# Loading q in one transfer with 32 token groups outermost, in a fused retention and token-mixing kernel

## The chip, the cores and the metric

The kernel runs on one core of one Trainium2 chip. The metric is the device time of one execution in microseconds (us), as the median of several runs. A separate execution was taken by the hardware profiler; its rows are used to see where the time goes.

## What is computed

Inputs are q, k and v, each of shape 4 x 8 x 768 x 64 (batch, heads, tokens, head width) in 32-bit floats, and three weights. All of q, k and v are 6.29 MB each.

```python
# retention: one decaying 64x64 state per batch and head
for t in range(S):
    state = gamma[h] * state + outer(k[:, :, t], v[:, :, t])
    y[:, :, t] = q[:, :, t] @ state / sqrt(D)
x = y.transpose(0, 2, 1, 3).reshape(B, S, H * D)      # 4 x 768 x 512
# token mixing: the weights over tokens come from x itself
W_tok = (x @ w_q) @ (x @ w_k).T / sqrt(d_hyper)        # per batch, no softmax
out = relu(W_tok @ x) @ w_out                          # 4 x 768 x 512
```

Because there is no softmax, the kernel forms `z = (x @ w_k).T @ x` per batch and multiplies `x @ w_q` with it.

## The kernel before

The work is cut into 12 pairs. A pair is 256 tokens of one batch, two chunks (c = 0, 1) of 128 tokens, and three pairs make a batch. For each pair the steps are: loads of k, v and q; casts to bf16 (`ck`, `cv` with the decay multiplied in, `cq`); transposes of k and q on TensorE into PSUM (`trk`, `trq`) and their evictions (`ek`, `eq`); scores k times q (`sc`), evicted with a causal mask (`eat`); the product with v (`ia`); the product of q with the carried state (`in`, `ic`); the state update (`st`, `es`); the eviction of y with its decay (`ex`); the transpose of x (`xt`, `exT`); the products with w_q and w_k (`wqk`, evicted by `ew`); z (`zm`, `ez`); the mix (`mx`, relu in `r`); the output projection (`pj`, evicted by `eo`); and the store.

Two lists written out by hand set the order. `ORDER` lists every step with its engine (A is ScalarE, V is VectorE, P is GpSimd) and its PSUM bank, and each engine runs its own steps strictly in that order. `LOADS` lists the transfers in the order in which SyncE issues them, all but the first half of k of pair 0: first the loads of all pairs, then all stores. A staging pool has 16 buffers of 512 KB; the load that reuses a buffer waits until the tensor before it is cast. The q of a pair is the 2nd, 5th, 6th, ... entry, and the last loads are `k11 q11 v10 v11`.

A q load (line 151) is two transfers, one for the even and one for the odd heads. In each, the four heads of that parity are outermost, then 32 groups of 8 neighbouring tokens, then 8 x 64 floats, which are 2 KB in a row in DRAM. So partition 32 w + g holds head pair w and token group g. The k and v loads (lines 159 and 167) have 128 token groups or tokens outermost, with rows of 512 bytes (types 1 and 2) or 256 bytes (type n, the last three pairs). After `trq`, eight transposes of 128 x 128, the columns of the transposed q come in the order (w, c, j, group), with j the token within its group, so that each head pair's 128 tokens of a chunk lie in a row for the score matmuls. Tokens are then handled in the order (j, group) in all later steps, and a store (line 823) writes 128 rows of 2 KB per chunk with the 8 values of j outermost, one transfer for each chunk.

The transposed q has two uses on TensorE: as the moving operand of the scores (lines 496 and 514), and as the stationary operand, loaded as weights, of the products with the state (lines 554, 580 and 599).

Of the kernel before, what the change touches and what calls it, by code (L numbers as in the profile page):

```python
# [10 lines left out]
BF16 = mybir.dt.bfloat16  # L11
# [56 lines left out]
def kernel(  # L68
# [13 lines left out]
    nc = tc.nc  # L82
# [3 lines left out]
    DH = moe_w_q.shape[1]  # L86
    C = 128
# [4 lines left out]
    HP = H // 2  # L92
    J = 8
    QG = C // J

    wk_scale = (1.0 / math.sqrt(D)) ** 3 / math.sqrt(DH)
# [3 lines left out]
    def pool(name, bufs, **kw):  # L100
        return ctx.enter_context(tc.tile_pool(name=name, bufs=bufs, **kw))
# [7 lines left out]
    kq_pool = pool("kq", KQS)  # L109
# [9 lines left out]
    def bank32(b, n=1):  # L119
        return banks[:, b : b + n, :].rearrange("p n f -> p (n f)")  # L120

    def bank16(b):
        return banks[:, b, :].bitcast(BF16)

    pairs = [dict() for _ in range(NG)]
# [4 lines left out]
    ENGINES = {"A": nc.scalar, "V": nc.vector, "P": nc.gpsimd}  # L130

    def copy(e, out, in_):
        if e == "A":
            return nc.scalar.copy(out=out, in_=in_)  # L134
        return ENGINES[e].tensor_copy(out=out, in_=in_)  # L135

    def rows(i):
        return slice(i * 64, i * 64 + 64)

    def halves(half):  # L140
        return slice(0, HP) if half is None else slice(half * HP // 2, (half + 1) * HP // 2)

    def load(name, p, half=None, eng=None):
        src = {"k": k, "q": q, "v": v}[name]
        b, cp = divmod(p, NP)
        st = pairs[p]
        t0 = cp * 2 * C
        if name == "q":
            st["q_st"] = stage_pool.tile([128, 2, J, D], FP32, name="q_st", tag="st")
            for x in range(2):  # L150
                nc.sync.dma_start(  # L151
                    out=st["q_st"][:, x].rearrange("p j d -> p (j d)"),
                    in_=src[b, x::2, t0 : t0 + 2 * C, :].rearrange("w (g j) d -> w g (j d)", j=J),
                )
            return
        if TYPES[p] == "n":
            st[name + "_st"] = stage_pool.tile([128, 2, HP, 2, D], FP32, name=name + "_st", tag="st")
            for c in range(2):
                (eng or nc.sync).dma_start(  # L159
                    out=st[name + "_st"][:, c].rearrange("t hp x d -> t (hp x) d"),  # L160
                    in_=src[b, :, t0 + c * C : t0 + (c + 1) * C, :].rearrange("h t d -> t h d"),
                )
            return
        if name + "_st" not in st:
            st[name + "_st"] = stage_pool.tile([128, HP, 2, 2, D], FP32, name=name + "_st", tag="st")
        hs = halves(half)
        (eng or nc.sync).dma_start(
            out=st[name + "_st"][:, hs].rearrange("g hp x j d -> g (hp x) (j d)"),
            in_=src[b, 2 * hs.start : 2 * hs.stop, t0 : t0 + 2 * C, :].rearrange(
                "h (g j) d -> g h (j d)", j=2  # L170
            ),
        )

    wstages = {}
# [18 lines left out]
    def load_token(token):  # L193
        if token[0] in "wo":
            load_weights(token)
        else:
            load(token[0], int(token[1:]))

    load("k", 0, 0, nc.scalar)
    load("k", 0, 1, nc.sync)  # L200

    queue = list(LOADS)
# [19 lines left out]
    def release(token, n):  # L222
        parts[token] = parts.get(token, 0) + 1
        if parts[token] == n:
            cast.add(token)
            more_loads()
# [14 lines left out]
        out=pt[:, 1:2], in0=pt[:, 0:1], scalar1=4, scalar2=None, op0=ALU.arith_shift_right  # L241
    )
    nc.vector.tensor_scalar(
        out=pt[:, 2:3], in0=pt[:, 0:1], scalar1=15, scalar2=3,
# [19 lines left out]
    for x in range(2):  # L264
# [11 lines left out]
        out=ty.rearrange("p n x c h -> p (n x c h)"),  # L276
        in0=ty.rearrange("p n x c h -> p (n x c h)"),
# [7 lines left out]
    if "2" in TYPES:  # L285
        fy2 = const_pool.tile([128, NP, 2, HP, 2], FP32, name="fy2")
        for cp in range(NP):
            nc.vector.tensor_copy(
                out=fy2[:, cp], in_=fy[:, cp].rearrange("p x c hp -> p c hp x")
            )  # L290

    if "n" in TYPES:
# [10 lines left out]
            out=tn.rearrange("p n c h -> p (n c) h"),  # L303
            in0=tn.rearrange("p n c h -> p (n c) h"),
# [32 lines left out]
    wqk_sb = const_pool.tile([128, NDM, 3 * DH], BF16, name="wqk_w")  # L337
    wout_sb = const_pool.tile([128, NDM, DM], BF16, name="wout_sb")

    def W(e):  # L340
        copy(
            e,
            wqk_sb[:, :, 0 : 2 * DH].rearrange("p a (r h) -> p a r h", r=2),
            wstages["w"][:, 0][:, :, None, :].to_broadcast([128, NDM, 2, DH]),
        )
        wk_stage = wstages["w"][:, 1]
        if e == "A":
            nc.scalar.mul(out=wqk_sb[:, :, 2 * DH :], in_=wk_stage, mul=float(wk_scale))
        else:
            ENGINES[e].tensor_scalar_mul(  # L350
                out=wqk_sb[:, :, 2 * DH :], in0=wk_stage, scalar1=float(wk_scale)
            )
        release("w", 1)

    def WO(e, b, i):
# [114 lines left out]

    def trq(e, b, p):
        st = pairs[p]
        ps = bank16(b).rearrange("p (n j g) -> p n j g", j=J, g=QG)
        for j in range(J):
            nc.tensor.transpose(  # L475
                ps[:, :, j], st["qs"][:, j].rearrange("p x d -> p (x d)"), identity
            )
        st["qT_ps"] = bank16(b)

    def eq(e, b, p):  # L480
        st = pairs[p]
        st["qT"] = kq_pool.tile([128, HP, 2, J, QG], BF16, name="qT")
        copy(e, st["qT"].rearrange("p w c j g -> p (w c j g)"), st["qT_ps"])

    def qT(p, x, hp, c):
        return pairs[p]["qT"][rows(x), hp, c].rearrange("p j g -> p (j g)")

    def sc1(e, b, p, half):
        st = pairs[p]
# [223 lines left out]

    def wqk(e, b, p):
        st = pairs[p]
        wk_ps = bank32(b)[:, 0:128].rearrange("p (c n) -> p c n", c=2)
        wq_ps = bank32(b)[:, 128:384]
        for c in range(2):
            for a in range(NDM):
                nc.tensor.matmul(  # L720
                    out=wk_ps[:, c, :],
                    lhsT=st["xT"][:, a, c, :],
                    rhs=wqk_sb[:, a, 2 * DH :],
                    start=(c == 0 and a == 0),
                    stop=(a == NDM - 1),
                    skip_group_check=True,
                )
        for a in range(NDM):
            nc.tensor.matmul(  # L729
                out=wq_ps,  # L730
                lhsT=wqk_sb[:, a, 0 : 2 * DH],
                rhs=st["xT"][:, a].rearrange("p c t -> p (c t)"),
                start=False,
                stop=(a == NDM - 1),
                skip_group_check=True,
            )
        st["wqk_ps"] = bank32(b)[:, 0:384]

    def ew(e, b, p):
        st = pairs[p]  # L740
        w = moe_pool.tile([128, 384], BF16, name="wqk_n")
        copy(e, w, st["wqk_ps"])
        st["wk"] = w[:, 0:128].rearrange("p (c n) -> p c n", c=2)
        st["wqT"] = w[:, 128:384]

# [69 lines left out]
    def stored(name):  # L815
        p, _, c = name.partition("/")
        p, cs = int(p), [int(c)] if c else [0, 1]
        if not all((p, i) in evicted for i in cs):
            return False
        b, cp = divmod(p, NP)  # L820
        for i in cs:
            t0 = cp * 2 * C + i * C
            nc.sync.dma_start(
                out=out[b, t0 : t0 + C, :].rearrange("(g j) m -> j g m", j=J),
                in_=pairs[p]["o"][:, i],
            )
        return True

    steps2 = dict(
        ck=ck2, cv=cv2, cq=cq, trk=trk, ek=ek, trq=trq, eq=eq, sc=sc2, eat=eat, st=state2, es=es, ia=ia2,  # L830
        **{"in": inter2}, ic=cross2, ex=ex2, xt=xt, exT=exT, wqk=wqk, ew=ew, zm=zm, ez=ez, mx=mx, r=r, pj=pj, eo=eo,
        WO=WO,
    )
# [5 lines left out]
    for token in ORDER:  # L839
        token, _, b = token.partition("@")  # L840
        token, _, e = token.partition(":")
        name, *args = token.split(".")
        args = [int(i) for i in args]
        if name == "fence":
            fence(e, int(b))
        elif name == "fill":
            fill(args[0], int(b))
        elif name == "W":
            W(e)
        elif name == "mask":  # L850
            masks("12n"[args[0]])
        else:
            steps = steps1 if name in ("ez", "WO") else kinds[TYPES[args[0]]]
            steps[name](e, int(b) if b else None, *args)
# [30 lines left out]
```

## Time and profile before

| | |
|---|---|
| median of 3 runs | 152.17 us (152.16 to 152.41) |
| the profiled execution's own time | 153.09 us |
| its span, first to last instruction | 151.4 us |
| TensorE (PE) busy | 97.2 us |
| VectorE (DVE) busy | 75.1 us |
| ScalarE (ACT) busy | 64.1 us |
| GpSimd (POOL) busy | 63.2 us |
| mean granted TensorE clock | 0.80 of full speed |

No engine is busy for two thirds of the span. The granted clock is a share of 2.4 GHz, and a stretch has either 0.5 (1.2 GHz) or 1.0, so means lie between. In the rows, "idle before" is an engine's idle time just ahead of an instruction, with what ended it. The DMA share is the mean busy share of the core's 16 DMA engines, so 0.25 can be four engines at full work, and it can read slightly above 1 in a short window.

### The profile page before, as it was taken

How to read it: one execution, taken by the hardware profiler on the slowest of the kernel's cores; microseconds unless marked ns; L12 is line 12 of the kernel's file. 1: busy time of each engine (PE TensorE's matmuls, PEld its weight loads, DVE VectorE, ACT ScalarE, POOL GpSimd, SP SyncE). 2: the span in 40 equal slices, each digit the busy share in tenths (PEclk: the TensorE clock that was granted, in tenths of full speed). 3: DMA queues.
4: the chain of work that ended last, by engine and by line, in shares of the span. 5: the costliest groups of instructions: out<-in, count | busy, mean ns of one | idle time of the engine just before them, and what ended most of it. 6: DMA issues, size and time to landing. Idle time of an engine off the chain costs nothing. (4 is left out here: it accounts for less than half of the span.)

```text
span 151.4 us, 3451 instructions
## 1 busy us (share of the span) xinstructions
PE 97.2 (64%) x1429; PEld 70.4 (47%) x1439; DVE 75.1 (50%) x107; ACT 64.1 (42%) x101; POOL 63.2 (42%) x87
## 2 busy tenths in 40 slices
PE   6704714582693990899719943994466999999200
PEld 2204613572672880677516632663355777644000
DVE  4008423454764291459629980577050896666000
ACT  4306321614762651358227771471250775534300
POOL 7605970092842941971939425970509400000000
PEclk9965555567558599569999999699786999999975
DMA  3766266466766696562635475955448555555551
GB/s 103 206 187 191 109 187 197 129 224 166 205 197 181 210 296 180 171 191 102 191 115 183 138 209 140 254 147 140 125 145 185 177 194 197 201 199 204 205 204 74
DMA packets 39263, 26.69 MB, mean 176 GB/s; under 512 B 14160, under 2 KB 32592, under 8 KB 39248
## 3 DMA queue, kind: packets, MB, share of 16 engines
q1 hardware_dynamic: 38720, 26.22, 57.3%
q10 hardware_dynamic: 528, 0.26, 0.6%
q8 instruction: 11, 0.18, 0.5%
q14 instruction: 4, 0.03, 0.1%
HBM read 20.19 MB, written 6.29 MB: 175 GB/s over the span
## 5 line engine op out<-in xcount | busy, mean ns | idle before, releaser
L414 POOL TENSOR_TENSOR vs<-v_st,fv 64x512 bf16<-64x512 f32 x24 | 26.6, 1107 | 16.5 <-DMA v_st<-in_v_dram 15.2
L475 PE MATMUL banks<-identity,qs 128*128 128x128 bf16 x96 | 10.1, 269 | 32.4 <-POOL qs L135 17.1
L796 PE MATMUL banks<-wout_sb,relu 128*128 128x512 bf16 x86 | 23.1, 391 | 1.1 <-issue 0.8
L475 PEld LDWEIGHTS <-qs 128*128 128x128 bf16 x96 | 7.7, 122 | 34.7 <-POOL qs L135 18.3
L528 DVE TENSOR_TENSOR at_sb<-banks,cmask 128x1024 bf16<-128x1024 f32 x18 | 21.5, 1217 | 2.5 <-PE banks L496 1.3
L135 POOL CAST qs<-q_st 128x1024 bf16<-128x1024 f32 (+1 forms) x8 | 7.0, 877 | 32.9 <-DMA q_st<-in_q_dram 28.8
L692 DVE TENSOR_TENSOR x_nat<-banks,fy 128x1024 bf16<-128x1024 f32 x10 | 12.2, 1221 | 9.7 <-PE banks L648 9.6
L134 ACT CAST qs<-q_st 128x512 bf16<-128x512 f32 x7 | 4.3, 619 | 29.4 <-DMA q_st<-in_q_dram 29.4
L134 ACT COPY o_st<-banks 128x512 f32<-128x512 f32 x19 | 11.1, 586 | 11.5 <-PE banks L796 11.4
L135 POOL CAST ks<-k_st 64x512 bf16<-64x512 f32 (+1 forms) x21 | 13.4, 643 | 4.3 <-DMA k_st<-in_k_dram 3.7
L451 PE MATMUL banks<-identity,ks 128*128 128x128 bf16 x96 | 11.1, 280 | 6.1 <-POOL ks L135 4.7
L796 PEld LDWEIGHTS <-relu 128*128 128x128 bf16 x96 | 8.6, 101 | 8.9 <-issue 1.4
L451 PEld LDWEIGHTS <-ks 128*128 128x128 bf16 x96 | 8.6, 128 | 8.0 <-POOL ks L135 5.2
L789 ACT ACTIVATE relu<-banks 128x1024 bf16<-128x1024 f32 x9 | 9.2, 1027 | 7.1 <-PE banks L774 7.1
L135 DVE CAST qs<-q_st 128x512 bf16<-128x512 f32 x4 | 1.7, 427 | 18.9 <-DMA q_st<-in_q_dram 18.9
L134 ACT CAST ks<-k_st 64x512 bf16<-64x512 f32 (+2 forms) x12 | 7.8, 652 | 6.5 <-POOL ks L135 5.0
L134 ACT COPY kT<-banks 128x1024 bf16<-128x1024 bf16 x8 | 8.1, 1012 | 5.1 <-PE banks L451 5.1
L134 ACT COPY qT<-banks 128x1024 bf16<-128x1024 bf16 x7 | 7.1, 1011 | 5.9 <-PE banks L475 5.6
L648 PE MATMUL banks<-vs,at_sb 128*128 128x64 bf16 x160 | 9.1, 213 | 0.0
L496 PE MATMUL banks<-qT,kT 64*128 64x128 bf16 x160 | 8.5, 248 | 0.8 <-DVE qT L135 0.8
L704 PE MATMUL banks<-identity,x_nat 128*128 128x128 bf16 x96 | 8.9, 247 | 0.0
L729 PE MATMUL banks<-xT,wqk_w 128*128 128x256 bf16 x48 | 8.3, 302 | 0.0
(80 smaller groups left out, 164.2 us busy)
## 6 DMA issues: line engine op xcount, KB each, us to landing
q_st<-in_q_dram SPq DMA_DIRECT2D x24, 256.0 KB
out_dram<-o_st SPq DMA_DIRECT2D x24, 256.0 KB
v_st<-in_v_dram SPq DMA_DIRECT2D x9, 512.0 KB
k_st<-in_k_dram SPq DMA_DIRECT2D x8, 512.0 KB
k_st<-in_k_dram SPq DMA_DIRECT2D x7, 256.0 KB
v_st<-in_v_dram SPq DMA_DIRECT2D x6, 256.0 KB
o_st<-in_moe_w_out_dram SPq DMA_DIRECT2D x2, 512.0 KB
k_st<-in_k_dram ACTq DMA_DIRECT2D x1, 256.0 KB
```

What stands on the lines that cost most here:

```text
L134: return nc.scalar.copy(out=out, in_=in_)
L135: return ENGINES[e].tensor_copy(out=out, in_=in_)
L414: ENGINES[e].tensor_tensor(out=st["vs"][rows(j), c].rearrange("p hp x d -> p (hp x) d"), in0=st["v_st"][rows(c), :, :, j].rearrange("p hp ...
L451: nc.tensor.transpose(ps[:, hp, i], src.rearrange("p x d -> p (x d)"), identity)
L475: nc.tensor.transpose(ps[:, :, j], st["qs"][:, j].rearrange("p x d -> p (x d)"), identity)
L496: nc.tensor.matmul(out=ps[:, x, hi, c, :], lhsT=st["kT"][rows(x), hp, c, :], rhs=qT(p, x, hp, c), start=(hi == 0 and c == 0), stop=(hi == ...
L528: ENGINES[e].tensor_tensor(out=st["at", half].rearrange("p x hi i t -> p (x hi i t)").rearrange("p (m n) -> p m n", n=n), in0=st["at_ps", ...
L648: nc.tensor.matmul(out=y[:, x, c, hp, :], lhsT=st["at", half][:, x, hi, c, :], rhs=st["vs"][:, c, hp, x, :], start=first(p, x), stop=False ...
L692: nc.vector.tensor_tensor(out=st["x"].rearrange("p c hp x d -> p x (c hp) d"), in0=st["y_ps"].rearrange("p x c hp d -> p x (c hp) d"), in1 ...
L704: nc.tensor.transpose(ps[:, a, c], st["x"][:, c, a].rearrange("p x d -> p (x d)"), identity)
L789: nc.scalar.activation(out=dst, in_=st["mx_ps"], func=ACT.Relu)
L796: nc.tensor.matmul(out=bank32(b), lhsT=st["relu"][:, a, c, :], rhs=wout_sb[:, a, :], start=(a == 0), stop=(a == NDM - 1),)
```

## The change

The two q transfers become one, with the 32 token groups outermost and the eight heads behind them. Partition 4 g + w then holds token group g and head pair w. The transposed q comes out in the order (c, j, group, w): the four head pairs are interleaved, and the columns of one head pair stand four bf16 elements (8 bytes) apart. The evictions in `eq` stay contiguous copies, while the score matmuls and the state products read the transposed q with that step.

The eviction `ew` writes the tokens back into natural order, reading PSUM with a step of 16 floats. For wk this goes with a reordering of the columns of w_k in `W` and an output of eight-float pieces in `wqk`. The stores then write tokens in natural order: 128 tokens outermost, and both chunks in one transfer for pairs 0 to 8, where 24 store transfers become 15.

```diff
--- before.py
+++ after.py
@@ -147,11 +147,10 @@
         t0 = cp * 2 * C
         if name == "q":
             st["q_st"] = stage_pool.tile([128, 2, J, D], FP32, name="q_st", tag="st")
-            for x in range(2):
-                nc.sync.dma_start(
-                    out=st["q_st"][:, x].rearrange("p j d -> p (j d)"),
-                    in_=src[b, x::2, t0 : t0 + 2 * C, :].rearrange("w (g j) d -> w g (j d)", j=J),
-                )
+            nc.sync.dma_start(
+                out=st["q_st"].rearrange("p x j d -> p x (j d)"),
+                in_=src[b, :, t0 : t0 + 2 * C, :].rearrange("h (g j) d -> g h (j d)", j=J),
+            )
             return
         if TYPES[p] == "n":
             st[name + "_st"] = stage_pool.tile([128, 2, HP, 2, D], FP32, name=name + "_st", tag="st")
@@ -343,13 +342,12 @@
             wqk_sb[:, :, 0 : 2 * DH].rearrange("p a (r h) -> p a r h", r=2),
             wstages["w"][:, 0][:, :, None, :].to_broadcast([128, NDM, 2, DH]),
         )
-        wk_stage = wstages["w"][:, 1]
+        wk_stage = wstages["w"][:, 1].rearrange("p a (h1 h0) -> p a h0 h1", h0=J)
+        wk_sb = wqk_sb[:, :, 2 * DH :].rearrange("p a (h0 h1) -> p a h0 h1", h0=J)
         if e == "A":
-            nc.scalar.mul(out=wqk_sb[:, :, 2 * DH :], in_=wk_stage, mul=float(wk_scale))
+            nc.scalar.mul(out=wk_sb, in_=wk_stage, mul=float(wk_scale))
         else:
-            ENGINES[e].tensor_scalar_mul(
-                out=wqk_sb[:, :, 2 * DH :], in0=wk_stage, scalar1=float(wk_scale)
-            )
+            ENGINES[e].tensor_scalar_mul(out=wk_sb, in0=wk_stage, scalar1=float(wk_scale))
         release("w", 1)
 
     def WO(e, b, i):
@@ -470,7 +468,7 @@
 
     def trq(e, b, p):
         st = pairs[p]
-        ps = bank16(b).rearrange("p (n j g) -> p n j g", j=J, g=QG)
+        ps = bank16(b).rearrange("p (c j n) -> p c j n", c=2, j=J)
         for j in range(J):
             nc.tensor.transpose(
                 ps[:, :, j], st["qs"][:, j].rearrange("p x d -> p (x d)"), identity
@@ -479,11 +477,11 @@
 
     def eq(e, b, p):
         st = pairs[p]
-        st["qT"] = kq_pool.tile([128, HP, 2, J, QG], BF16, name="qT")
-        copy(e, st["qT"].rearrange("p w c j g -> p (w c j g)"), st["qT_ps"])
+        st["qT"] = kq_pool.tile([128, 2, J * QG, HP], BF16, name="qT")
+        copy(e, st["qT"].rearrange("p c t w -> p (c t w)"), st["qT_ps"])
 
     def qT(p, x, hp, c):
-        return pairs[p]["qT"][rows(x), hp, c].rearrange("p j g -> p (j g)")
+        return pairs[p]["qT"][rows(x), c, :, hp]
 
     def sc1(e, b, p, half):
         st = pairs[p]
@@ -713,7 +711,7 @@
 
     def wqk(e, b, p):
         st = pairs[p]
-        wk_ps = bank32(b)[:, 0:128].rearrange("p (c n) -> p c n", c=2)
+        wk_ps = bank32(b)[:, 0:128].rearrange("p (h0 c h1) -> p c h0 h1", h0=J, c=2)
         wq_ps = bank32(b)[:, 128:384]
         for c in range(2):
             for a in range(NDM):
@@ -739,7 +737,11 @@
     def ew(e, b, p):
         st = pairs[p]
         w = moe_pool.tile([128, 384], BF16, name="wqk_n")
-        copy(e, w, st["wqk_ps"])
+        copy(
+            e,
+            w.rearrange("p (i g j) -> p i g j", i=3, j=J),
+            st["wqk_ps"].rearrange("p (i j g) -> p i g j", i=3, j=J),
+        )
         st["wk"] = w[:, 0:128].rearrange("p (c n) -> p c n", c=2)
         st["wqT"] = w[:, 128:384]
 
@@ -818,11 +820,13 @@
         if not all((p, i) in evicted for i in cs):
             return False
         b, cp = divmod(p, NP)
-        for i in cs:
-            t0 = cp * 2 * C + i * C
+        if c:
+            t0 = (2 * cp + cs[0]) * C
+            nc.sync.dma_start(out=out[b, t0 : t0 + C, :], in_=pairs[p]["o"][:, cs[0]])
+        else:
             nc.sync.dma_start(
-                out=out[b, t0 : t0 + C, :].rearrange("(g j) m -> j g m", j=J),
-                in_=pairs[p]["o"][:, i],
+                out=out[b, cp * 2 * C : (cp + 1) * 2 * C, :].rearrange("(c t) m -> t c m", c=2),
+                in_=pairs[p]["o"],
             )
         return True
```

## Rows read from the trace of the kernel before

**Rows 1.** The page: busy time of each engine, and TensorE's clock in 40 slices.

```profile
PE 97.2 (64%) x1429; PEld 70.4 (47%) x1439; DVE 75.1 (50%) x107; ACT 64.1 (42%) x101; POOL 63.2 (42%) x87
...
PEclk9965555567558599569999999699786999999975
```

**Rows 2.** The chain that ended last: start us, us, what.

```profile
105.84 7.84 DMA q_st<-in_q_dram
...
113.83 1.05 POOL qs L135
...
140.87 0.59 ACT o_st L134
```

**Rows 3.** Waits: engine, line, releaser; us in total, times, longest.

```profile
PE banks L475 <- POOL qs L135: 17.1, 5, 4.4
...
PE banks L475 <- ACT qs L134: 9.0, 2, 5.7
...
PE banks L475 <- DVE qs L135: 6.3, 2, 3.3
...
PE banks L451 <- POOL ks L135: 4.7, 2, 4.0
```

**Rows 4.** The q staging tile: idle time of casting engines, and what ended it.

```profile
  DMA q_st<-in_q_dram: 77.2, 17
```

**Rows 5.** Windows of 1 to 1.4 us: busy, clock, DMA share, GB/s.

```profile
53.00:54.00 1.00, 1.00 (x21) 0.95 (x20) 1.00 (x2) 0.00 (x0) 0.94 (x2) 0.91 1.05 332
91.00:92.00 1.00, 0.00 (x0) 0.00 (x0) 0.00 (x0) 0.00 (x0) 0.00 (x0) 1.00 0.27 90
93.00:94.00 1.00, 0.57 (x9) 0.56 (x10) 0.00 (x0) 0.00 (x0) 0.67 (x2) 1.00 1.03 236
146.00:147.00 1.00, 0.00 (x0) 0.00 (x0) 0.00 (x0) 0.00 (x0) 0.00 (x0) 0.50 0.52 203
150.00:151.40 1.40, 0.00 (x0) 0.00 (x0) 0.00 (x0) 0.00 (x0) 0.00 (x0) 0.50 0.00 0
```

**Rows 6.** SyncE's queue late on: start us, us, line, transfer, count.

```profile
102.52 3.85 SPq L151 DMA_DIRECT2D q_st<-in_q_dram  x2
106.47 7.97 SPq L159 DMA_DIRECT2D v_st<-in_v_dram  x4
```

**Rows 7.** Windows by stage; columns PE, PEld, DVE, ACT, POOL, clock, share, GB/s.

```profile
6.70:11.60 4.90, 0.00 (x0) 0.00 (x0) 0.00 (x0) 0.00 (x0) 0.02 (x1) 0.71 0.64 173
11.60:113.80 102.20, 66.31 (x1082) 51.97 (x1088) 56.41 (x63) 46.67 (x71) 52.68 (x59) 0.76 0.61 175
80.00:90.00 10.00, 8.75 (x165) 6.01 (x164) 9.46 (x10) 8.30 (x15) 5.64 (x6) 1.00 0.52 164
113.80:141.46 27.66, 25.45 (x332) 16.55 (x336) 16.90 (x18) 14.25 (x24) 5.09 (x5) 0.94 0.57 195
141.46:151.40 9.94, 0.00 (x0) 0.00 (x0) 0.00 (x0) 0.00 (x0) 0.00 (x0) 0.70 0.40 154
```

**Rows 8.** ScalarE's timeline at the start: k's first load and its cast.

```profile
0.79 0.48 ACTq L167 DMA_DIRECT2D k_st<-in_k_dram  x1
...
5.06 1.24 ACT L134 CAST ks<-k_st 64x512 bf16<-64x512 f32 x2 [1.23 <-DMA k_st<-in_k_dram]
```

**Rows 9.** Groups by form: busy us, mean ns of one, idle before.

```profile
L451 PE MATMUL banks<-identity,ks 128*128 128x128 bf16 x96 | 11.1, 280 | 6.1 <-POOL ks L135 4.7 <-ACT qT L134 1.1 <-ACT ks L134 0.4
...
L475 PE MATMUL banks<-identity,qs 128*128 128x128 bf16 x96 | 10.1, 269 | 32.4 <-POOL qs L135 17.1 <-ACT qs L134 9.0 <-DVE qs L135 6.3
...
L496 PE MATMUL banks<-qT,kT 64*128 64x128 bf16 x160 | 8.5, 248 | 0.8 <-DVE qT L135 0.8
...
L720 PE MATMUL banks<-wqk_w,xT 128*128 128x64 bf16 x96 | 5.6, 208 | 0.0
...
L134 ACT CAST wqk_n<-banks 128x384 bf16<-128x384 f32 x11 | 5.1, 481 | 3.5 <-PE banks L729 3.3
...
L554 PEld LDWEIGHTS <-qT 64*128 64x128 bf16 x128 | 3.7, 109 | 0.7 <-issue 0.2
...
L514 PE MATMUL banks<-qT,kT 64*64 64x128 bf16 x64 | 1.8, 266 | 0.1
```

## The prediction

> **What bounds the kernel now.** I read the page first. PE, the busiest engine, works 97.2 us of a span of 151.4, and its clock falls to half in many slices [rows 1], so something starves all engines at once. The chain of waits names it: the last q lands at 113.7, is cast at 113.83, and from there the work runs without a hole to the last eviction, which ends at 140.87 + 0.59 = 141.46 [rows 2]. The waits say how often this happens. PE stands still ahead of the q transposes nine times, for 17.1 + 9.0 + 6.3 = 32.4 us, and its largest other stall is 4.0 us for a k cast on POOL (`ck.10`), which is queued behind the cast of q [rows 3]. The casting engines waited 17 times for q's data, 77.2 us in all [rows 4].
>
> Why q is late is seen in short windows [rows 5]. At 53 to 54 us all 16 DMA engines are busy and move 332 GB/s. At 91 to 92 every compute engine waits for a q, the DMA share is 0.27 and 90 GB/s flow: four engines. At 146 to 147 only stores are left, with a share of 0.52 and 203 GB/s: eight engines, 25 GB/s each. The count follows the outermost dimension of the access pattern: the four heads of one parity in a q load, the eight j in a store, 128 in the k and v loads. The sum by engine agrees. All of q's 6.29 MB passes through four engines, 1.57 MB each; the stores add 6.29/8 = 0.79 and the rest 13.9/16 = 0.87. That makes 3.23 MB on each of these four, 127 us at 25.4 GB/s, which fills most of the span, while an engine outside the first eight carries 0.87 MB. SyncE's queue is backed up behind them: two q issues take 3.85 us, four v issues 7.97 [rows 6], so k and v come late as well.
>
> **The change, part by part.** *The q load.* With 32 groups outermost on one side and 128 partitions on the other, I expect 16 engines, as 4, 8 and 128 gave 4, 8 and 16. No row shows a load with 32, so four engines stays a rival. With q and the stores spread, each engine carries 26.5/16 = 1.66 MB. One issue in place of two also removes 12 instructions from SyncE's queue; I count nothing for that, since its time is waiting for room.
>
> Three gains follow. First, the start. From 6.7 to 11.6 us no compute engine works [rows 7], waiting for q0. The first k, 0.52 MB in two halves, is issued at 0.79 and cast at 5.06 [rows 8]. A q of 0.52 MB behind it needs 1.6 us at 332 GB/s or 2.2 at 236, the slowest rate of a window with all engines busy [rows 5], so 6.7 to 7.3. I take 7.0, a gain of 4.6.
>
> Second, the stretch from q0's cast to q11's, 102.2 us [rows 7]. If data is there in time, PE loses its stalls for q: 32.4 less the first of 5.7, which is in the gain above, is 26.7, and the 4.0 for `ck.10` makes 30.7. It leaves 71.5 us. In it PE would be busy 66.3, most of it priced at a clock of 0.76, DVE 56.4, POOL 52.7 and ACT 46.7 [rows 7]. So DVE works 79% of the time. What is late next is DVE (score masks, evictions of y) and PE's waits for it. The best that rows allow is DVE's densest stretch, 9.46 of 10 us: 56.4/0.946 = 59.6, which is 11.9 less. I keep 71.5: it takes away only PE's stalls for q, and gains from a warmer PE are set against waits that now come to light.
>
> Are the loads then in time? Up to q11 the loads are 20.2 - 1.05 = 19.1 MB (v10 and v11 follow). Behind k0, at 332 GB/s they end 56 us after 5.06, at 61; at 236 GB/s 79 us after, at 84. The forecast wants q11 at 7.0 + 71.5 = 78.5, so they fit at any rate above 253 GB/s. The low end is a rival below.
>
> Third, the tail. From the last eviction at 141.46 to the end pass 9.94 us [rows 7], because stores still queue on eight engines. With loads done by 80 and 16 engines, the 6.29 MB of stores need 16 us at twice 203 GB/s, during the 27.7 us that PE works after q11's cast, which I leave as they are. The last store of 256 KB then goes alone. Its price is that of the first loads, 5.06 - 0.79 = 4.3, and the 1.4 us at the end in which nothing moves [rows 5]: 5.7, a gain of 4.2.
>
> *The interleaved q.* Where `qT` is the moving operand there are 224 score matmuls, busy 8.5 + 1.8 = 10.3 us. Where it is loaded as weights, 128 loads take 3.7, so all 176 take 5.1 [rows 9]. No row shows PE reading with a step. Below nothing is excluded, since the columns are as many; above I set a doubling, fully exposed: 15.4 us. I take nothing, being nearest to the same instructions as they stand, and keep 15.4 for the range. The Trainium skill's page "SBUF — State Buffer", section "Door 1: The DMA port swizzle", says that SBUF has 16-byte lines and that two hits on a line suffice for full bandwidth. A step of 8 bytes gives just two, so by it the price is nothing; no run here shows it yet.
>
> *PSUM writes in pieces.* `trq` now writes runs of 64 bf16 in place of 16, and the 96 matmuls of `wqk` for wk write runs of eight floats. The row for pieces exists: `trq` in runs of 32 bytes takes 269 ns against 280 for `trk`, which writes whole rows [rows 9]. So I price it at nothing. The Trainium skill speaks against this part: the page "PSUM — Partial Sum Buffer", section "Specifications (TRN2)", says that any non-contiguous access slows matmuls significantly. The two rows do not bear that out for runs of 32 bytes; doubling the 5.6 us of line 720 by it would add 5.6 and give 118.3.
>
> *`ew` and `W`.* Twelve evictions of 481 ns now read with a step. Doubled, they add 5.8 us, nearly all to ACT, which works 64.1 us [rows 1, 9] of some 112; nothing of it is on the path as long as ACT has that slack. `W`'s product runs once on POOL, ahead of work that waits for loads: nothing.
>
> **The sum.** 151.4 - 4.6 - 30.7 - 4.2 = 111.9 us of span. The profiled execution took 153.09, 1.69 more than its span, and the median of the runs is 0.92 below that, so I add 0.77: 112.7.
>
> **The rivals.**
> - *The loads stay the bound.* If the mix of 256- and 512-byte rows holds the 16 engines at 236 GB/s throughout, q11 lands at 84 in place of 78.5, and the end comes 5.3 us later: 118. For it speaks that the 12.6 MB of k and v come in such rows; against it that windows with all engines busy also show 332.
> - *The step costs PE twice.* 112.7 + 15.4 = 128. Against it: PE has 5 us free in the stretch, and some would be hidden.
> - *Slower.* The step costs so much that PE becomes the bound by itself. The gain to be eaten is 152.2 - 112.7 = 39.5 us over 400 instructions, 99 ns each; a score matmul now has 46 ns of busy time and a load 29. At four times the price they add 30.9 + 15.3 = 46.2, and the time is 159. Nothing in the trace speaks for it, and nothing excludes it.
> - *The load stays on four engines.* Then only the tail gains its 4.2 us: 148. Against it: the counts of 4, 8 and 16.
>
> **How the numbers follow.** The forecast's case, with DVE and PE the next bound and 101 to 118 as its own range (from 112.7 - 11.9), gets 0.70. The loads at their low rate get 0.12, the doubled step 0.10, four engines 0.04, slower 0.04. The predicted time is 112.7. The range reaches from 101 to 128, which takes in the second and third; past it lie the last two and some of the first. All cases but the last are faster: 0.95. A change within 0.2%, about what these runs can tell from none, gets 0.01, and slower 0.04.
>
> **What the profile afterwards would show.** Right: no window with a share near 0.27 while all engines wait; DMA at 250 GB/s or more until the loads end at 60 to 85 us; PE's idle time ahead of line 475 below 10 us; under 6.5 us after the last eviction; lines 496 and 554 at their old durations per clock; `trq` no dearer. Wrong would be: q windows still at a quarter of the engines; line 496 or 554 at twice its time; or new waits of PE for DVE or POOL that eat the 30.7 us, the likeliest way to miss within the range's upper half.

## The result, and the profile after

The median falls from 152.29 us (4 runs, 152.16 to 153.25) to 103.27 (4 runs, 101.66 to 105.57), a ratio of 0.670 with a 95% interval of 0.663 to 0.678. All ratios here are of the fast runs alone, without those over 1.5% above the fastest of the same kernel, so that they differ a little from the quotient of the medians (0.678). The profiled execution took 102.75 us with a span of 101.0. The forecast was 112.7 with a range of 101 to 128: the direction and the range hold, with the measured time near the range's lower end, and the gain is 49.0 us where 39.6 were forecast.

The page of the changed kernel answers to [rows 1]: busy time of each engine, TensorE's clock and the DMA share in 40 slices, the chain that ended last by engine, and, from its last part, the q loads and the stores of one chunk (count, size, median us from issue to landing).

```profile
PE 90.5 (90%) x1439; PEld 64.5 (64%) x1439; DVE 75.4 (75%) x107; ACT 63.7 (63%) x101; POOL 63.2 (62%) x87
...
PEclk9999555589999999999999999999999999999999
DMA  0999999998999999999998999999935000522983
...
PE 71%; DVE 7%; DMA 7%; issue 4%; ACT 3%; POOL 3%; SPq 1%; DVEq 0%; POOLq 0%
...
q_st<-in_q_dram SPq DMA_DIRECT2D x12, 512.0 KB, 6.8
...
out_dram<-o_st SPq DMA_DIRECT2D x6, 256.0 KB, 2.0
```

The DMA engines are now full in nearly all slices until 70 us and then mostly idle, because the loads are over and the stores wait for results; the digit 9 at 93 us is of stores alone. DVE, ACT and POOL do the same work as before. PE needs 90.5 us in place of 97.2: its clock is at half in four slices at the start and full from then on.

The windows by stage answer to [rows 7]; the columns are the same. The first row runs from q0's cast to q11's, the second to the end of the last eviction, the third to the end.

```profile
7.16:65.15 57.99, 52.23 (x961) 40.75 (x960) 50.10 (x57) 41.96 (x64) 52.63 (x59) 0.91 1.08 316
65.15:98.07 32.92, 32.30 (x467) 21.64 (x465) 23.47 (x25) 18.61 (x31) 5.09 (x6) 1.00 0.54 194
98.07:101.00 2.93, 0.00 (x0) 0.00 (x0) 0.00 (x0) 0.01 (x1) 0.00 (x0) 1.00 0.46 179
12.50:22.00 9.50, 8.72 (x141) 7.65 (x141) 7.59 (x9) 5.77 (x10) 8.94 (x10) 0.56 1.12 349
40.00:50.00 10.00, 9.91 (x201) 7.53 (x198) 9.19 (x12) 7.40 (x12) 9.03 (x11) 1.00 1.10 369
50.00:60.00 10.00, 10.00 (x172) 7.03 (x170) 9.12 (x10) 7.64 (x14) 9.44 (x11) 1.00 1.05 248
```

The first stretch shrank from 102.2 to 58.0 us, and all 16 DMA engines move 316 GB/s in it, where it was 175. From 40 to 60 us four things are at or near their limit together: PE works 99 to 100% of the time, DVE 91 to 92%, POOL 90 to 94%, and the DMA share reads 1.05 to 1.10. No single bound is left there, though PE leads: the chain that ended last runs over it for 71% of the span. In the second stretch PE works without a hole, 32.3 of 32.9 us. That stretch is longer than the 27.7 us of before, since POOL casts q11 while PE still has 467 matmuls to go, where it had 332.

The q staging tile answers to [rows 4], and the groups by form to [rows 9].

```profile
  DMA q_st<-in_q_dram: 6.6, 4
```

```profile
L494 PE MATMUL banks<-qT,kT 64*128 64x128 bf16 x160 | 12.0, 288 | 1.2 <-DVE qT L135 0.8 <-ACT kT L134 0.3
...
L473 PE MATMUL banks<-identity,qs 128*128 128x128 bf16 x96 | 8.1, 234 | 0.3 <-ACT qs L134 0.3
...
L449 PE MATMUL banks<-identity,ks 128*128 128x128 bf16 x96 | 7.9, 230 | 0.7 <-DVE at_sb L526 0.7
...
L134 ACT CAST wqk_n<-banks 128x384 bf16<-128x384 f32 x11 | 5.1, 482 | 2.7 <-PE banks L727 2.5
...
L718 PE MATMUL banks<-wqk_w,xT 128*128 128x64 bf16 x96 | 4.8, 193 | 0.0
...
L552 PEld LDWEIGHTS <-qT 64*128 64x128 bf16 x128 | 3.7, 115 | 0.3
...
L512 PE MATMUL banks<-qT,kT 64*64 64x128 bf16 x64 | 2.4, 289 | 0.2 <-DVE x_nat L690 0.2
```

The casting engines wait 6.6 us for q in place of 77.2, and PE 0.3 us ahead of the q transposes in place of 32.4. Most PE groups became cheaper at the higher clock, `trk` from 11.1 to 7.9 us, but the scores, whose moving operand is the transposed q, rose from 8.5 + 1.8 to 12.0 + 2.4 us. The step in the operand is not free.

### The profile page after: what moved, and what is told of

Same layout as the page of the kernel before. It is cut to its first block, busy times and chain, and to the rows that moved or that the text cites. A ratio compares the mean times of both kernels' runs of the same rounds, so it can differ in the third digit from the quotient of the medians.

```text
span 101.0 us, 3421 instructions
## 1 busy us (share of the span) xinstructions
PE 90.5 (90%) x1439; PEld 64.5 (64%) x1439; DVE 75.4 (75%) x107; ACT 63.7 (63%) x101; POOL 63.2 (62%) x87
## 4 chain that ended last, share of the span: by engine, by line
PE 71%; DVE 7%; DMA 7%; issue 4%; ACT 3%; POOL 3%; SPq 1%; DVEq 0%; POOLq 0%
PE banks L798 19%; PE banks L494 10%; DMA v_st<-in_v_dram 7%; PE banks L646 5%; PE banks L727 5%; PE banks L449 5%; PE banks L473 5%; PE banks L702 4%; PE banks L611 4%; POOL vs L412 3%; PE banks L718 3%; PE banks L756 3%; PE banks L776 2%; PE banks L552 2%; DVE qT L135 2%
## 5 line engine op out<-in xcount | busy, mean ns | idle before, releaser
L134 ACT COPY o_st<-banks 128x512 f32<-128x512 f32 x19 | 11.1, 586 | 12.0 <-PE banks L798 11.7
L494 PE MATMUL banks<-qT,kT 64*128 64x128 bf16 x160 | 12.0, 288 | 1.2 <-DVE qT L135 0.8
L494 PEld LDWEIGHTS <-kT 64*128 64x128 bf16 x160 | 7.9, 107 | 2.8 <-issue 1.9
L611 PE MATMUL banks<-vs,ks 128*64 128x64 bf16 x144 | 5.9, 208 | 3.1 <-POOL vs L412 3.1
L449 PE MATMUL banks<-identity,ks 128*128 128x128 bf16 x96 | 7.9, 230 | 0.7 <-DVE at_sb L526 0.7
L473 PE MATMUL banks<-identity,qs 128*128 128x128 bf16 x96 | 8.1, 234 | 0.3 <-ACT qs L134 0.3
L646 PE MATMUL banks<-vs,at_sb 128*128 128x64 bf16 x160 | 8.0, 201 | 0.0
L526 DVE TENSOR_TENSOR at_sb<-banks,cmask_n 128x1024 bf16<-128x1024 f32 x6 | 7.2, 1219 | 0.9 <-PE banks L494 0.7
L134 ACT CAST s_sb<-banks 128x256 bf16<-128x256 f32 x16 | 6.0, 375 | 2.9 <-PE banks L611 1.7
L611 PEld LDWEIGHTS <-ks 128*64 128x64 bf16 x144 | 4.2, 117 | 5.6 <-issue 4.6
L727 PE MATMUL banks<-xT,wqk_w 128*128 128x256 bf16 x48 | 7.2, 273 | 0.3 <-issue 0.3
```

The lines of the kernel that those rows point to most:

```text
L449: nc.tensor.transpose(ps[:, hp, i], src.rearrange("p x d -> p (x d)"), identity)
L473: nc.tensor.transpose(ps[:, :, j], st["qs"][:, j].rearrange("p x d -> p (x d)"), identity)
L494: nc.tensor.matmul(out=ps[:, x, hi, c, :], lhsT=st["kT"][rows(x), hp, c, :], rhs=qT(p, x, hp, c), start=(hi == 0 and c == 0), stop=(hi == ...
L526: ENGINES[e].tensor_tensor(out=st["at", half].rearrange("p x hi i t -> p (x hi i t)").rearrange("p (m n) -> p m n", n=n), in0=st["at_ps", ...
L611: nc.tensor.matmul(out=state_ps[rows(x), hp, :], lhsT=st["ks"][:, c, hp, x, :], rhs=st["vs"][:, c, hp, x, :], start=(cp == 0 and c == 0 an ...
L646: nc.tensor.matmul(out=y[:, x, c, hp, :], lhsT=st["at", half][:, x, hi, c, :], rhs=st["vs"][:, c, hp, x, :], start=first(p, x), stop=False ...
```

## The experiments

The theory: four DMA engines on q were the whole brake, and what is left is shared by PE, DVE, POOL and the loads. Its rivals: the gain is that of one transfer in place of two, of the layout, or of the stores; or PE's price for the step now sets the time.

**Engines without layout (e1_four).** The kernel before, with q in four transfers.

```diff
-            for x in range(2):
-                nc.sync.dma_start(out=st["q_st"][:, x]..., in_=src[b, x::2, ...]...("w (g j) d -> w g (j d)"))
+            for w in range(HP):
+                nc.sync.dma_start(
+                    out=st["q_st"][32 * w : 32 * w + 32].rearrange("p x j d -> p x (j d)"),
+                    in_=src[b, 2 * w : 2 * w + 2, t0 : t0 + 2 * C, :].rearrange("h (g j) d -> g h (j d)", j=J),
+                )
```

> The kernel before, with one edit: q is loaded in four transfers, one for each head pair, each with 32 token groups outermost. The layout of q, the contiguous operands on TensorE, the token order and the stores stay as before. Theory (the number of DMA engines of a q load sets the pace): no window with a DMA share near 0.27 is left, all loads are done by 75 us, and the time is 98 to 107 us, with the score matmuls at their old 0.40 us for eight at full clock. Rival (the gain comes from the single transfer or from the interleaved layout): 140 us or more, as neither is here and SyncE issues 24 transfers more than before.

Measured: 115.55 us (four runs, 113.75 to 117.76) against 153.4 for before, so some 38 us of gain with no change in layout, token order or stores, and with more transfers. The rivals of one transfer and of the layout fall as explanations of most of the gain. But the forecast for it was too low, for two reasons that its windows show (q0's cast to q11's, to the last eviction, to the end).

```profile
7.60:77.28 69.68, 54.52 (x1064) 42.04 (x1065) 54.25 (x62) 44.80 (x69) 53.38 (x60) 0.93 1.04 263
77.28:105.26 27.98, 27.35 (x363) 18.15 (x360) 18.41 (x20) 16.07 (x27) 5.04 (x5) 0.94 0.57 197
105.26:113.90 8.64, 0.00 (x0) 0.00 (x0) 0.00 (x0) 0.00 (x0) 0.00 (x0) 0.66 0.41 158
```

The share is as full (1.04) but moves 263 GB/s in place of 316, so q11 is cast at 77.3 and not at 65.2, with the casting engines waiting 19.9 us for q where those of the changed kernel wait 6.6; and the old stores leave a tail of 8.6 us.

**Partitions in one transfer (e9_step4 and e7_two).** Both load q in two transfers of 256 KB with 32 groups outermost. The first writes partitions 0 to 63 and then 64 to 127, the second all 128 partitions twice.

```diff
+            for w in range(2):          # e9_step4
+                nc.sync.dma_start(
+                    out=st["q_st"][64 * w : 64 * w + 64].rearrange("p x j d -> p x (j d)"),
+                    in_=src[b, 4 * w : 4 * w + 4, t0 : t0 + 2 * C, :].rearrange("h (g j) d -> g h (j d)", j=J),
+                )
+        st["qT"] = kq_pool.tile([128, 2, 2, J * QG, 2], BF16, name="qT")
...
+            for x in range(2):          # e7_two
+                nc.sync.dma_start(
+                    out=st["q_st"][:, x].rearrange("p j d -> p (j d)"),
+                    in_=src[b, x::2, t0 : t0 + 2 * C, :].rearrange("w (g j) d -> g w (j d)", j=J),
+                )
```

> The changed kernel, with q in two transfers of four heads and 64 partitions each, both with 32 token groups outermost, so that only two head pairs are interleaved: a step of 4 bytes in place of 8. Theory (the price of the step goes by its bytes; 16 engines are what the loads need): eight score matmuls take 0.40 to 0.50 us; the loads stay on 16 engines, with a rate between that of one transfer (316 GB/s until q11's cast) and that of four (some 250); 100 to 105 us. Rival (one transfer of 128 partitions is what counts): the loads fall back and the time is 107 us or more.

> The changed kernel, with q in two transfers again, for even and odd heads as before, but each with the 32 token groups outermost. Theory (the outermost dimension sets the number of engines, and all 128 partitions are written by each transfer): the loads keep their rate, and the time is within 1.5 us of the control. Rival (one transfer in place of two is part of the gain): at least 3 us above the control.

Measured: 107.5 us for the first (before, measured beside it: 152.77), past the range of its theory and within that of its rival, and 102.14 for the second beside 102.66 for the changed kernel itself, repeated as a control.

> The changed kernel itself, unedited, on the same chip as the next three, since its runs differ by more than those of before: 101 to 105 us.

The rows from q0's cast to q11's, first of e9_step4, with the wait of its casting engines for q:

```profile
7.04:75.93 68.89, 55.72 (x1066) 42.57 (x1067) 54.29 (x62) 44.91 (x69) 53.58 (x59) 0.93 1.06 267
...
  DMA q_st<-in_q_dram: 20.9, 13
```

and of e7_two:

```profile
6.90:66.87 59.97, 53.98 (x981) 41.72 (x980) 51.12 (x58) 42.81 (x66) 53.24 (x59) 0.94 1.03 304
```

Two transfers in place of one cost nothing. With two transfers of 64 partitions for each q, all transfers of the stretch together move only 267 GB/s, much as with four of 32, and the casts wait for q again. The two kernels have the same number and size of transfers, so the count and the size are not it; what differs is the partitions that each covers and, with them, which heads it reads and whether a partition gets one row of 2 KB or two. No run separates these. The Trainium skill's page "SBUF — State Buffer", section "Door 1: The DMA port swizzle", says that partitions 0 to 63 cover only eight of SBUF's sixteen ports and no more than 0 to 31 do. The likeness of 267 and 263 GB/s agrees with that, but no run here shows ports.

**Each half of the change alone (e3_oldstores, e4_stores).** The first is the changed kernel with token order, `W`, `wqk`, `ew` and stores of before; the second has those of the change, with q loaded, transposed and evicted as before.

```diff
-            nc.sync.dma_start(out=out[b, ...].rearrange("(c t) m -> t c m", c=2), in_=pairs[p]["o"])
+        for i in cs:                    # e3_oldstores; e4_stores undoes the q load, trq, eq and qT instead
+            nc.sync.dma_start(out=out[b, t0 : t0 + C, :].rearrange("(g j) m -> j g m", j=J), in_=pairs[p]["o"][:, i])
```

> The changed kernel, with the token order and the stores of before: one transfer for each chunk, the 8 values of j outermost. Theory (the q loads are nearly all of the gain; the stores only set the tail): stores run at a share near 0.5 and 203 GB/s, 31 us for all of them from 65 us on, the end of the compute stays where it is, and the tail after the last eviction grows from 2.9 us to 4 to 9: 103 to 109 us. Rival (the stores hold back the whole): 115 us or more.

> The kernel before, with the changed kernel's token order and stores, and q loaded and laid out as before. Theory (the q loads hold the kernel): q11 is still cast near 114 us, compute ends near 141, and only the tail shrinks, from 9.9 to about 3 us: 145 to 148 us. Rival (the stores are a large part of the gain): under 135 us.

Measured: 109.24 us (ratio 0.706, 0.701 to 0.711) and 146.55 (0.947, 0.942 to 0.953), the first just past its theory's range and the second within it. By the ratios the q half alone is worth 0.294 of the time before and the store half 0.053, together 0.347; the whole change gave 0.330 and the control 0.334. Alone they give some 2 us more than together, little more than the intervals allow, so they nearly add up and neither needs the other. The four engines on q were most of the brake, not the whole. The stores' half is the tail: here the last rows of the windows, of e3_oldstores

```profile
97.71:106.10 8.39, 0.00 (x0) 0.00 (x0) 0.00 (x0) 0.00 (x0) 0.00 (x0) 0.76 0.43 165
```

and of e4_stores.

```profile
11.46:113.96 102.50, 68.77 (x1088) 53.04 (x1088) 55.63 (x63) 46.72 (x71) 53.12 (x60) 0.72 0.61 174
113.96:140.23 26.27, 24.55 (x336) 15.40 (x336) 16.82 (x18) 14.27 (x24) 5.05 (x5) 1.00 0.68 244
140.23:143.20 2.97, 0.00 (x0) 0.00 (x0) 0.00 (x0) 0.00 (x0) 0.00 (x0) 1.00 0.46 177
```

Compute ends at 97.7 with the old stores, no later than with the new ones, and 8.4 us follow in place of 2.9. With the new stores alone the stretch between the casts stays at 102.5 us.

**What the step costs TensorE (e2_deint, e8_read, e5_step16).** The first two take the step out of TensorE's operand, by writing with a step in `eq` or by reading PSUM with one; the third doubles it to 16 bytes.

```diff
+        st["qT"] = kq_pool.tile([128, HP, 2, J * QG], BF16, name="qT")
+        copy(e, st["qT"].rearrange("p w c t -> p c t w"),                     # e2_deint
+             st["qT_ps"].rearrange("p (c t w) -> p c t w", c=2, w=HP))
...
+        copy(e, st["qT"].rearrange("p w c t -> p w (c t)"),                   # e8_read
+             st["qT_ps"].rearrange("p (n w) -> p w n", w=HP))
...
+        st["qT"] = kq_pool.tile([128, 2, J * QG, 2 * HP], BF16, name="qT")    # e5_step16
+        copy(e, st["qT"][:, :, :, 0:HP].rearrange("p c t w -> p (c t) w"),
+             st["qT_ps"].rearrange("p (n w) -> p n w", w=HP))
```

> The changed kernel, with the eviction of the transposed q writing each head pair's columns in a row, so that TensorE reads both operands without a step; the eviction itself writes with a step instead. Theory (the 8-byte step costs TensorE about 0.22 us for eight score matmuls at full clock, some 4 us in all, and TensorE is now the bound): eight score matmuls go back from 0.62 to 0.40 us and the time falls by 2 to 4 us against the changed kernel, to 99 to 101 us, if the evictions keep 1.0 us on ScalarE and stay under 1.3 us on VectorE. Rival (the longer score matmuls are hidden): the time stays at 102 to 104 us.

> The changed kernel, with the eviction of the transposed q reading PSUM with a step of 8 bytes and writing each head pair's columns in a row, so that TensorE reads without a step and no engine writes with one. Theory (TensorE is the bound and pays about 4 us for the step): if the evictions stay near 1.0 us on ScalarE and under 1.3 us on VectorE, eight score matmuls take 0.40 us again and the time falls by 2 to 4 us, to 99 to 101 us. Rival (the step on TensorE is hidden): no change against the changed kernel, 102 to 104 us. If a stepped read costs an eviction as much as a stepped write did (4.77 us), the time is 130 us or more.

> The changed kernel, with the columns of one head pair 16 bytes apart in the transposed q in place of 8: the eviction leaves every second group of four elements empty. The output is the same. Theory (what the score matmuls pay goes by how many of their columns share a line of SBUF): eight score matmuls take clearly more than the 0.62 us at 8 bytes, about 0.9 to 1.2 us, and the time grows by 4 to 10 us, to 107 to 114 us. Rival (any step costs the same): 0.62 us and 102 to 105 us, with the evictions as they were.

Measured: 134.89, 101.87 and 114.7 us. The first tells nothing of TensorE's price in the total, because its own copies became far dearer, which I had not expected. Two groups of e2_deint by form:

```profile
L134 ACT COPY qT<-banks 128x1024 bf16<-128x1024 bf16 x7 | 33.4, 4766 | 6.6 <-PE banks L473 6.6
...
L135 DVE COPY qT<-banks 128x1024 bf16<-128x1024 bf16 x5 | 23.9, 4774 | 2.4 <-PE banks L473 1.5 <-PE banks L556 0.8
```

Neighbouring elements written 512 bytes apart cost 4.77 us on either engine, where the plain copy takes 1.01 and 0.69. Reading PSUM with 8 bytes between elements costs ScalarE nothing and VectorE half a microsecond, as the same groups of e8_read show, with its scores:

```profile
L498 PE MATMUL banks<-qT,kT 64*128 64x128 bf16 x160 | 7.8, 226 | 3.1 <-DVE qT L135 1.3 <-DVE xT L135 0.7 <-DVE at_sb L530 0.7
...
L134 ACT COPY qT<-banks 128x1024 bf16<-128x1024 bf16 x7 | 7.1, 1013 | 2.3 <-PE banks L473 2.2
L135 DVE COPY qT<-banks 128x1024 bf16<-128x1024 bf16 x5 | 6.1, 1216 | 1.1 <-PE banks L556 0.8 <-PE banks L473 0.2
```

So the price of the step on PE is known: 12.0 + 2.4 us of score matmuls fall to 7.8 + 1.5, some 5 us, and PE's whole busy time from 90.5 (88.9 in the control) to 84.4. The timelines give it by step. Eight score matmuls at full clock, late in each kernel:

| step between columns | 2 bytes (before, e8_read) | 4 (e9_step4) | 8 (changed) | 16 (e5_step16) |
|---|---|---|---|---|
| us for eight | 0.40 | 0.40 | 0.62 | 1.07 |

One row for each step, of before, e9_step4, the changed kernel and e5_step16:

```profile
120.27 0.40 PE L496 MATMUL banks<-qT,kT 64*128 64x128 bf16 x8
...
70.62 0.40 PE L495 MATMUL banks<-qT,kT 64*128 64x128 bf16 x8
...
79.99 0.62 PE L494 MATMUL banks<-qT,kT 64*128 64x128 bf16 x8
...
60.82 1.07 PE L498 MATMUL banks<-qT,kT 64*128 64x128 bf16 x8
```

At half clock the step of 8 bytes is nearly free. A row of the timeline for 16 of them, of the kernel before

```profile
16.42 1.04 PE L496 MATMUL banks<-qT,kT 64*128 64x128 bf16 x16
```

and of the changed kernel, at half clock and then at full clock:

```profile
12.45 1.09 PE L494 MATMUL banks<-qT,kT 64*128 64x128 bf16 x16
...
51.04 1.08 PE L494 MATMUL banks<-qT,kT 64*128 64x128 bf16 x16
```

The same two rows of e5_step16:

```profile
12.25 1.99 PE L498 MATMUL banks<-qT,kT 64*128 64x128 bf16 x16
...
56.67 1.98 PE L498 MATMUL banks<-qT,kT 64*128 64x128 bf16 x16
```

With a step of 8 or 16 bytes 16 score matmuls take the same time at either clock. So 1.09 us for them in a timeline does not tell the clock; without the step they take 1.04 at half clock and 0.62 at full.

The time says less than the busy time: e8_read has a ratio of 0.668 (0.663 to 0.673) and the changed kernel 0.670. What PE saves is hidden. VectorE's longer copies take 2.7 us more, and from 40 to 60 us VectorE now works 95 to 96% of the time, as these windows of e8_read show; that this is what hides it is argued, not shown.

```profile
40.00:50.00 10.00, 9.92 (x214) 7.47 (x209) 9.51 (x12) 7.58 (x13) 9.07 (x11) 1.00 1.08 360
50.00:60.00 10.00, 9.26 (x175) 6.32 (x172) 9.58 (x10) 7.64 (x14) 9.42 (x11) 1.00 0.86 205
```

At 16 bytes the price shows: PE's busy time rises to 101.7 us and the kernel by 11 us, so there PE is the bound.

**What is left of PE's price and of its cold start (e10_fill, e12_mixed, e13_mixed_fill).** e12_mixed reads PSUM with the step only where ScalarE evicts. The fills put matmuls on zeros into a gap of PE, ahead of a stretch at half clock; their results are not used.

```diff
+        if e == "A":   # e12_mixed: as e8_read; else: as the changed kernel
...
-... cv.1.0:P trk.0@6 cv.1.1:P ...
+... cv.1.0:P trk.0@6 fill.12@3 cv.1.1:P ...      # e10_fill; e13_mixed_fill is e12_mixed with fill.18@3
```

> The changed kernel, with 12 more matmuls on zeros, into an otherwise unused bank, between the first k transpose and the first state update, where TensorE waits 3.1 us for v and after which its clock is at half until 21 us. Theory (the time that the forecast missed is TensorE's clock): the clock stays full or is half for less long in this stretch, the matmuls from 12 to 21 us take about half, and the time falls by 1 to 4 us. Rival (the stretch is set by loads and casts, and the clock there costs nothing): within 1 us of the changed kernel.

> The changed kernel, with the eviction of the transposed q reading PSUM with the step only where ScalarE does it (7 of 12 pairs; it costs ScalarE nothing), while VectorE keeps its contiguous copy and leaves the step to TensorE. Theory (TensorE's price for the step is partly on the path, and VectorE's longer copies took back some of what their removal gave): 0.5 to 3 us below the control. Rival (the step is hidden altogether): within 0.5 us of the control.

> The kernel of the mixed evictions, with 18 matmuls on zeros between the first k transpose and the first state update, where 12 left the clock to fall at 12.7 us. Theory (the half clock at the start costs time on the path): the clock stays full through 12 to 22 us and the time falls by another 1 to 4 us. Rival (that stretch goes by casts and loads): within 1 us of the kernel with mixed evictions alone.

Measured: 102.1, 101.47 and 101.05 us. The ratios to before are 0.666 (0.662 to 0.670) for the control, 0.657 (0.652 to 0.661) for e12_mixed and 0.659 (0.656 to 0.663) for e13_mixed_fill. So e12_mixed may gain some 1.2 us, 1% of the time, but that PE's price for the step is on the path is not shown: e7_two, which pays it in full, has 0.662 (0.657 to 0.666), which overlaps both, and e8_read, which takes it away altogether, gained nothing. e10_fill missed its aim: the clock stayed full through the gap of 1.6 us behind the fill, to 13.5 us, and then was half until 20. Two of its windows:

```profile
12.40:13.40 1.00, 0.98 (x22) 0.94 (x23) 0.42 (x1) 0.00 (x0) 0.93 (x2) 1.00 1.04 400
13.60:20.00 6.40, 5.62 (x80) 4.80 (x76) 4.96 (x7) 4.16 (x6) 6.00 (x7) 0.50 1.12 355
```

The expectation of e13_mixed_fill has this fall at 12.7 us, where e10_fill's stepped scores take 1.09 us; but those take as long at full clock. e13_mixed_fill kept the clock full to about 17.9 us, as its PE timeline and two windows show (the scores at 16.80 are of a pair that VectorE evicts, so they read with the step):

```profile
7.81 4.05 PE L359 MATMUL banks<-warm 128*128 128x512 bf16 x18
12.34 0.32 PE L621 MATMUL banks<-vs,ks 128*64 128x64 bf16 x8 [0.48 <-POOL vs L412]
12.59 0.62 PE L504 MATMUL banks<-qT,kT 64*128 64x128 bf16 x16
...
16.80 1.09 PE L504 MATMUL banks<-qT,kT 64*128 64x128 bf16 x16 [1.11 <-DVE qT L135]
...
12.30:17.80 5.50, 3.61 (x72) 2.86 (x71) 4.93 (x7) 3.47 (x5) 5.13 (x6) 1.00 1.11 371
18.00:21.00 3.00, 3.00 (x47) 2.85 (x45) 2.05 (x3) 1.75 (x3) 2.81 (x4) 0.50 1.06 320
```

From 12.5 to 22 us PE works 7.65 us in place of 8.72, and the kernel is no faster for it: its interval overlaps that of e12_mixed. So the rival holds as far as a fill that reached half of the stretch can tell: that stretch goes by casts and loads (POOL works 8.94 of these 9.5 us).

## Why the prediction was right, and where a term was off

- **Cause and engines: right.** Four engines for q, eight for the stores, 16 for both afterwards. e1_four shows it with no change in layout or stores, e4_stores by keeping the four.
- **The start: right.** q0 is cast at 7.16 us, forecast 7.0.
- **From q0's cast to the last eviction: 8.3 us too long.** The forecast was 71.5 + 27.7 = 99.2, measured 58.0 + 32.9 = 90.9. The cut between the two parts was wrong as well: the forecast had q11's cast follow PE's pace, but POOL, which no longer waits for data there, casts it 32.9 us before the last eviction. For PE the sum can be split, to about 1 us, since ten of its 1439 matmuls have no record in the trace of before. Idle time: 129.9 - 91.8 = 38.1 before, less 30.7, gave 7.4; measured 90.9 - 84.5 = 6.4. So the stalls went as forecast, and the waits that I feared did not come. Busy time: 91.8 was kept; measured 84.5. The term that was off is "gains from a warmer PE are set against waits that now come to light": it kept PE at a clock of 0.76 and 0.94 in the two parts, and PE ran at 0.91 and 1.00. What the clock took off PE's busy time is more than these 7.2 us, since the interleaved operand added some 5: without it e8_read's PE needs 84.4 us of work at a clock of 0.966, e1_four's 87.4 at 0.914, e4_stores' 98.1 at 0.797 and before 97.2 at 0.800. This is bookkeeping on PE. It says where the 8.3 us lie, not that the clock alone is worth them: e8_read and e13_mixed_fill took some 5 and 1 us off PE's busy time and gained nothing, so other limits stand close behind PE, and how much the clock gave by itself stays open.
- **The tail: 2.8 us too long.** 2.93 where 5.7 were forecast. The first loads, with others in flight, were too dear a model for a last store alone; the page of the profile gives a median of 2.0 us from issue to landing for the 256 KB stores.
- **The sum.** 111.9 + 0.2 - 8.3 - 2.8 = 101.0, the span. The median lies 2.3 us above that where 0.8 were added, so the time was 9.4 us below the forecast.
- **The interleaved q: priced at nothing, which was wrong for the matmuls.** Score matmuls take 0.62 us for eight in place of 0.40. Some 5 us of PE's busy time came out of it; what of that reached the total is not clear of the noise (e12_mixed gains 1.2 us, e8_read nothing). The rival of a doubled price had the mechanism right for the matmuls, but most of it is hidden. By the rule of two hits on a line, from the Trainium skill's page "SBUF — State Buffer", section "Door 1: The DMA port swizzle", a step of 8 bytes would be free. The runs agree at half clock (1.04 and 1.09 us for 16) and not at full clock, where 4 bytes are free and 8 are not. The weight loads noticed less: 115 ns, where e8_read without the step takes 101.
- **PSUM in pieces, `ew` and `W`: right.** `trq` takes 234 ns beside 230 for `trk`, line 718 takes 193 ns beside 208, `ew` 482. The rule on non-contiguous access of the Trainium skill's page "PSUM — Partial Sum Buffer", section "Specifications (TRN2)", is again not borne out for runs of 32 bytes. `W`'s product went from 857 to 1427 ns (1104 to 1497 in the kernels with the new `W`), once in each. e3_oldstores, with the old `W`, ends its compute at 97.7 us where the changed kernel does at 98.1, so little of it can be on the path.
- **The loads in time: right.** 316 GB/s lies in the 236 to 332 that I had, and q11 was there before it was needed.

## What to carry to other kernels

Look for windows in which every engine waits and read the DMA share: here a share of 4/16 or 8/16 named a transfer whose outermost dimension is 4 or 8. Outermost dimensions of 32 and 128 used all 16 engines; nothing between 8 and 32 was tried. Let each transfer cover all 128 partitions, which went with the higher rate here. When stalls of TensorE go, reprice its work at the clock it will then have, and check what that leaves for the other engines: here PE, DVE, POOL and the loads met at once, and later savings on PE alone were worth little.

## What the runs showed of the hardware that I had not expected

- A moving operand with 8 bytes between bf16 columns costs 0.62 us for eight score matmuls at full clock against 0.40, with 16 bytes 1.07, and with 4 bytes no more than without a step. For 16 of them the stepped time is the same at half and at full clock: 1.09 and 1.08 us with 8 bytes, 1.99 and 1.98 with 16; without a step it is 1.04 and 0.62.
- Evictions that write neighbouring bf16 elements 512 bytes apart take 4.77 us for 1024 elements per partition on ScalarE and on VectorE. Reading PSUM with 8 bytes between elements takes 1.01 and 1.22, a plain copy 1.01 and 0.69.
- In the stretch from q0's cast to q11's, with all 16 engines busy, all transfers together move 267 and 263 GB/s where each q transfer covers 64 or 32 partitions, and 304 to 316 where it covers 128.
